# A fused attention and two-layer MoE kernel on one core: the weight projection moved into the key stage and spread over 32 blocks

## The chip, the core and the metric

The kernel runs on one core of a Trainium2 chip. The core has five engines that matter here: TensorE (PE, matrix products; its weight loads are shown as PEld), VectorE (DVE), ScalarE (ACT), GpSimd (POOL) and SyncE (SP, which here issues all DMAs). Every engine works through its own instructions in order and waits on semaphores for the others. On-chip data lie in SBUF; matrix products land in PSUM, eight banks per partition. The metric is the device time of one execution in microseconds (us), lower is better. The median of three runs of the kernel before is 1779.21 us (1768.62 to 1782.41).

## What is computed

Eight batches, eight heads, 576 positions, head size 64. A small set of 32 packed queries per head attends over the keys and values, the result is attended by the 576 queries, and the 4608 x 512 outcome goes through two feed-forward layers:

```python
p_packed = sm_attn(p, k, v)                # 32 x 64 per head
x = sm_attn(q, p_packed, p_packed)         # 576 x 64 per head
xn = x / sqrt(mean(x * x) + 1e-6) * rms_g  # x as 4608 x 512
g = xn @ w_gate
x1 = (g * sigmoid(g) * (xn @ w_val)) @ w_out      # d_ff 1536
h = x1 @ w2_in                                    # d_ff 2048
out = (h * cos(h)) @ w2_out
```

The weights arrive as 64-bit floats and are narrowed on the chip.

## The kernel before

The attention output of a batch is a 576 x 256 matrix of weights (softmax over 32 packed rows for 8 heads) times the packed values, so `xn @ w_gate` can be taken as (attention weights) x (packed values x w_gate). The product "packed values x weights" is the **projection**, `project` (L584). It makes, for each of 6 column chunks c, for gate and value (gv) and for each half of the heads (kt), a 128 x 4 x 256 piece for four batches at a time (bg = 0 is batches 0 to 3, bg = 1 is 4 to 7): 24 projections n of two **halves** (bg) each, 48 halves. A half is four matmuls into two PSUM tiles `mps`, one copy on ACT, one on DVE into an SBUF tile `ev` (4 buffers), and stores.

The program has these stages, one after the other in the order written (manual order up to the second layer):

- **Key stage** (loop over i = 0 to 17, two groups of four heads per batch): K and V are loaded ahead (`load_k(i + 3)`, `load_v(i + 2)`), POOL rearranges K (`u_copy`, L349, tile `kc`), PE transposes it (`u_kt`, tiles `kp`), scores `s` (`u_s1`), exponentials `e`, their transposes `et` (`u_et`), the packed values `pp` (`u_pp`), and their transposes `tp` (`u_fin`), which fill `ppT`, the projection's operand. Beside it 12 of the 24 pieces of w_gate and w_val (512 KB each, `wraw`, 3 buffers) and 4 pieces of w_out are loaded and narrowed in two parts, one iteration apart, and 26 of 43 steps of the attention of batch 0 (`bg0`) are interleaved.
- **First projections**: six of the 24 (both halves each), alternating with the rest of bg0.
- **Batch loop**: 24 blocks per batch (`gv_block`: 12 matmuls `gv` of gate and value; two blocks later `acc_block`: 12 matmuls `acc` into x1), with the attention of the next batch (`att_step`) interleaved. In batch 0 the 18 remaining projections run in the first blocks, one or two a block (`PJ_AT`), the last 12 weight pieces and 8 of w_out are loaded and narrowed there too, and batch 0 is taken in three segments of four d_ff blocks (`SEG`), whose partial sums of x1 go to DRAM and come back (`x1_load`). Batch 0's own part of a projection is copied straight into the SBUF tile `m0raw` by four 32 KB DMAs; everything else goes to `m_dram` and is read back per batch (`wm_load`), then split in two parts for the exact products (`wm_split`, tile `wmhl`, on ACT and POOL).
- **Second layer** (`h_block`, `o_block`), which the change does not touch.

Of the kernel before, what the change touches and what calls it, by code (L numbers as in the profile page):

```python
# [20 lines left out]
def kernel(  # L21
# [38 lines left out]
    BG_B, KP_B, ET_B, PP_B = 1, 2, 2, 1  # L60
    WRAW_B = 3
    WO_U = 4
    SEG, M0_D = 4, 0
    W_FROM, W_TO = 1, 14
    W_KV, W_B0 = 12, 12
    ATT_U, U_ATT, U_ATT_N = 26, 3, 2
    PJ_0, PJ_L, LATE_AT = 6, 0, 16
    PJ_AT = [7, 8] + [8 + x // 2 for x in range(1, 50)]
    EV_B = 4
    WM0_POOL = True  # L70
    W2_I0, W2_AT, W2_POOL = 25, (1, 3, 5, 7, 14, 18), False
    T_END, F3_B = 2, 3
    LAG, LAG_B = 2, 3
    WO_AT = {4: (-1, 0), 5: (1, 3), 6: (3, 6), 7: (6, 9), 8: (10, 12), 9: (13, 15), 10: (14, 17), 11: (16, 18)}
    M0_AT, M_AT = (16, 17, 18, 19, 20, 21), (3, 5, 7, 9, 11, 14)
    ATT_ORD = "t00 t01 x00 x01 x02 x03 t10 r00 t11 s00 x10 x11 p00 x12 p01 x13 - r10 - s10 - p10 p11"
    ATT_ORD0 = "t00 t01 x00 x01 x02 x03 r00 s00 p00 p01 t10 t11 x10 x11 x12 x13 r10 s10 p10 p11"
    AL_AT = 16
    X1_AT = {11: 0, 15: 1, 18: 0, 22: 1}
# [100 lines left out]

    gT = u1.tile([128, H], F32, name="gT")
    ppT = [mid_p.tile([128, H, 128], F32, name=f"ppT{i}") for i in range(B // 4)]
    pbd = [u1.tile([128, 2, 2 * NP], F32, name=f"pbd{i}") for i in range(2)]
    for t in pbd:
        nc.gpsimd.memset(t, 0.0)
# [142 lines left out]
    nat_k, nat_v, nat_c = {}, {}, {}  # L328
# [34 lines left out]
    def u_prep(i):  # L363
        pn, kc = nat_k.pop(i)[0], nat_c.pop(i)
# [3 lines left out]
        for r in range(2):  # L368
            rows = slice(r * 64, (r + 1) * 64)
            src, dst = (  # L370
                t[:, :, r * NP:(r + 1) * NP] for t in (pt[rows].rearrange("p (j x) -> p j x", j=2), pbd[i % 2][rows])
            )
            nc.vector.tensor_copy(dst, src)
        z["kT"], z["kc"] = u4.tile([128, 2, S], F32, tag="kT", name="kT"), kc

    def u_kt(i, js):
        z = st[i]
        kT, kc = z["kT"], z["kc"]
        for j in js:
            for hf in range(2):  # L380
                kp = ps_2.tile([128, HALF], F32, tag="kp", name="kp")
                for c in range(CH):
                    nc.tensor.transpose(
                        kp[:, c * CP:(c + 1) * CP],
                        kc[:, hf * CH + c, 2 * j:2 * j + 2, :].rearrange("p h d -> p (h d)"), ident[:CP, :CP],
                    )
                nc.scalar.activation(out=kT[:, j, hf * HALF:(hf + 1) * HALF], in_=kp, func=AF.Copy)

    def u_s1(i):
        z = st[i]  # L390
        kT = z["kT"]
        pb = pbd[i % 2]
        s1 = ps_1.tile([128, 2, 512], F32, tag="s1", name="s1")
        for hf in range(2):
            for j in range(2):
                nc.tensor.matmul(  # L396
                    s1[j * 64:(j + 1) * 64, hf, :HALF], pb[:, j], kT[:, j, hf * HALF:(hf + 1) * HALF],
                    start=True, stop=True,
                )
# [27 lines left out]
    def u_pp(i):  # L427
# [3 lines left out]
        pp = ps_1.tile([128, D], F32, tag="pp", name="pp", bufs=PP_B)  # L431
        for c in range(NC_):
            for h in range(4):
                r = slice(h * NP, (h + 1) * NP)
                nc.tensor.matmul(pp[r], eT[:, c, r], vn[:, h, c, :], start=c == 0, stop=c == NC_ - 1)
# [43 lines left out]
    def wy_prep(n, part):  # L479
        i, a = divmod(n, 2)  # L480
        c, gv = divmod(i, 2)
        if a == 0 and part == 0:
            w_y[i] = wm_p.tile([128, 4, 256], F32, tag="wm", name="wy")
# [522 lines left out]
```

## Time and profile before

| | |
|---|---|
| median of three runs | 1779.21 us |
| the profiled execution | 1776.91 us, its span 1775.1 us (1.8 us lie around it) |
| PE busy | 1696.1 us (96% of the span) |
| DVE, ACT, POOL busy | 1106.8, 863.8, 251.1 us |
| mean granted TensorE clock | 0.969 |

A busy PE is an engine with a matmul in flight, not an engine at its peak; the granted clock (1.00 is 2.4 GHz, and lower means are a mix with 1.2 GHz) and the idle time have to be read stage by stage.

### The profile page before, as it was taken

Reading aid. Unit: us, or ns where it says so; the run is one execution under the profiler, and the core shown is the slowest. Engines: PE = TensorE matmul, PEld = TensorE weight load, DVE = VectorE, ACT = ScalarE, POOL = GpSimd, SP = SyncE. Lnnn points to the kernel's source line nnn. Section 1 sums busy time; section 2 is a strip of 40 time slices with the busy share of each in tenths; the row PEclk is TensorE's granted clock in tenths of the full one; section 3 lists DMA queues with packets and bytes.
Section 4 is the critical chain, followed back from the end, with each engine's and each line's share of the span. In section 5 each row is a group of like instructions: output and inputs, shape, how many; then the busy total and the mean of one; then the engine's idle time right before and its main releaser. Section 6 shows DMA issues by size and latency. Waiting matters only on the chain.

```text
span 1775.1 us, 27791 instructions
## 1 busy us (share of the span) xinstructions
PE 1696.1 (96%) x10720; PEld 1495.0 (84%) x10720; DVE 1106.8 (62%) x2124; ACT 863.8 (49%) x1661; POOL 251.1 (14%) x202
## 2 busy tenths in 40 slices
PE   7787899799999999999999999999999999999999
PEld 4555677799999999999999888888888888888887
DVE  2565687557676767676656756565565656565554
ACT  4454454344444545454545645555554555454454
POOL 3331343412111111112122200000000000000000
PEclk9777899899999999999999999999999999999999
DMA  9995786553433334342223301010101000000000
GB/s 223 218 234 154 223 272 205 183 169 107 127 105 124 113 111 126 105 132 90 72 74 123 107 1 48 1 48 7 41 14 34 24 25 24 24 1 25 0 25 24
DMA packets 119981, 166.97 MB, mean 94 GB/s; under 512 B 26920, under 2 KB 84264, under 8 KB 119848
## 3 DMA queue, kind: packets, MB, share of 16 engines
q1 hardware_dynamic: 119848, 165.19, 32.1%
q8 instruction: 84, 1.38, 0.3%
q14 instruction: 49, 0.40, 0.1%
HBM read 108.79 MB, written 53.22 MB: 91 GB/s over the span
## 4 chain that ended last, share of the span: by engine, by line
PE 81%; DMA 6%; DVE 6%; issue 4%; ACT 2%; POOL 1%; SPq 0%; DVEq 0%; ACTq 0%; POOLq 0%
PE ops L154 7%; PE ops L152 7%; PE hp L153 7%; PE ops L153 7%; PE hp L152 7%; PE hp L154 7%; PE acc L152 5%; PE acc L153 5%; PE acc L154 5%; PE gv L152 5%; PE gv L154 4%; PE gv L153 4%; PE mps L595 2%; PE sp L235 1%; PE s L396 1%
## 5 line engine op out<-in xcount | busy, mean ns | idle before, releaser
L152 PE MATMUL gv<-apt,wmhl 128*128 128x288 f32 x768 | 234.3, 305 | 10.7 <-DVE silu L686 8.7
L152 PE MATMUL acc<-shl,wohl 128*128 128x288 f32 x768 | 237.4, 309 | 5.2 <-ACT wohl L104 5.0
L154 PE MATMUL acc<-shl,wohl 128*128 128x288 f32 x768 | 230.2, 300 | 0.5 <-POOL wohl L105 0.5
L153 PE MATMUL acc<-shl,wohl 128*128 128x288 f32 x768 | 230.3, 300 | 0.3 <-DVE shl L105 0.3
L154 PE MATMUL gv<-apt,wmhl 128*128 128x288 f32 x768 | 227.3, 296 | 1.0 <-POOL wmhl L105 1.0
L153 PE MATMUL gv<-apt,wmhl 128*128 128x288 f32 x768 | 227.6, 296 | 0.0
L152 PE MATMUL ops<-w2hl,ghl 128*128 128x512 f32 x576 | 224.2, 389 | 0.0
L153 PE MATMUL hp<-xhl,wmhl 128*128 128x512 f32 x576 | 224.1, 389 | 0.0
L154 PE MATMUL hp<-xhl,wmhl 128*128 128x512 f32 x576 | 224.1, 389 | 0.0
L153 PE MATMUL ops<-w2hl,ghl 128*128 128x512 f32 x576 | 224.1, 389 | 0.0
L152 PE MATMUL hp<-xhl,wmhl 128*128 128x512 f32 x576 | 224.1, 389 | 0.0
L154 PE MATMUL ops<-w2hl,ghl 128*128 128x512 f32 x576 | 222.7, 389 | 0.0
L926 DVE TENSOR_TENSOR r<-r,hp 128x512 f32<-128x512 f32 x144 | 98.9, 687 | 186.6 <-ACT r L925 186.6
L924 ACT ACTIVATE r<-r 128x512 f32<-128x512 f32 x144 | 91.0, 632 | 247.5 <-DVE r L923 247.5
L105 POOL TENSOR_TENSOR wmhl<-wmraw,wmhl 128x512 fp32r<-128x512 f32 x100 | 128.4, 1306 | 512.8 <-ACT wmhl L104 506.1
L104 ACT ACTIVATE shl<-silu 128x288 fp32r<-128x288 f32 x192 | 85.2, 444 | 231.9 <-DVE silu L687 230.7
L919 ACT ACTIVATE kk<-hp,magic 128x512 f32<-128x512 f32 x144 | 99.3, 689 | 122.6 <-PE hp L154 122.6
L152 PEld LDWEIGHTS gv<-apt,wmhl 128*128 128x128 f32 x768 | 145.5, 189 | 14.2 <-DVE silu L686 10.5
L152 PEld LDWEIGHTS acc<-shl,wohl 128*128 128x128 f32 x768 | 146.8, 191 | 10.8 <-ACT wohl L104 5.1
L153 PEld LDWEIGHTS acc<-shl,wohl 128*128 128x128 f32 x768 | 147.2, 192 | 0.6 <-DVE shl L105 0.5
L154 PEld LDWEIGHTS acc<-shl,wohl 128*128 128x128 f32 x768 | 146.6, 191 | 0.9 <-POOL wohl L105 0.9
L154 PEld LDWEIGHTS gv<-apt,wmhl 128*128 128x128 f32 x768 | 145.3, 189 | 1.5 <-POOL wmhl L105 1.5
(132 smaller groups left out, 3228.4 us busy)
## 6 DMA issues: line engine op xcount, KB each, us to landing
wmraw<-m SPq DMA_DIRECT2D x42, 512.0 KB
m<-ev SPq DMA_DIRECT2D x24, 512.0 KB, 4.2
x_dram<-x SPq DMA_DIRECT2D x40, 288.0 KB, 3.4
kn<-in_k_dram SPq DMA_DIRECT2D x16, 576.0 KB, 8.5
vn<-in_v_dram SPq DMA_DIRECT2D x16, 576.0 KB, 7.5
qnat<-in_q_dram SPq DMA_DIRECT2D x32, 288.0 KB, 6.2
m<-ev SPq DMA_DIRECT2D x24, 384.0 KB
x1raw<-x_dram SPq DMA_DIRECT2D x18, 512.0 KB, 3.9
```

The source lines that it names most:

```text
L104: nc.scalar.activation(out=hi, in_=src, func=AF.Copy)
L105: (eng or nc.vector).tensor_tensor(out=lo, in0=src, in1=hi.bitcast(F32), op=ALU.subtract)
L152: nc.tensor.matmul(ps, lhi, rhi, start=first, stop=False)
L153: nc.tensor.matmul(ps, lhi, rlo, start=False, stop=False)
L154: nc.tensor.matmul(ps, llo, rhi, start=False, stop=last)
L235: nc.tensor.matmul(sp[:, i, 2 * c:2 * c + 2, :], qT[:, i, c * CP:(c + 1) * CP], bq[:, 2 * j + i], start=True, stop=True,)
L396: nc.tensor.matmul(s1[j * 64:(j + 1) * 64, hf, :HALF], pb[:, j], kT[:, j, hf * HALF:(hf + 1) * HALF], start=True, stop=True,)
L595: nc.tensor.matmul(ps[r][:, j], ppT[bg][rows, 4 * kt + 2 * j + r], wy[rows, 2 * kt + j], start=True, stop=True)
L919: nc.scalar.activation(out=kk, in_=hp, func=AF.Identity, scale=1.0 / TWO_PI, bias=magic[:, 0:1])
L924: nc.scalar.activation(out=r, in_=r, func=AF.Abs)
L926: nc.vector.tensor_tensor(out=r, in0=r, in1=hp, op=ALU.mult)
```

## The change

It does six things.

1. The projection takes a half at a time. Twelve halves of bg = 0 (n = 0 to 11) run inside the key stage, in its iterations 10 to 16; the other 36 are spread over blocks 0 to 31 of the batch loop, one a block, two in blocks 4, 6, 8 and 10. The stage of first projections is gone.
2. For that the narrowed weights stay in SBUF until both halves are done, and the key stage loads 16 weight pieces in place of 12 (`W_KV`), with 4 buffers in place of 3 and both parts of the narrowing in the same iteration. Eight pieces are left for batch 0.
3. All of a half goes to `m_dram` by one 512 KB store, issued one step later (`store`); batch 0 reads its part back as other batches do. The `m0raw` copies are gone, and `ev` has 3 buffers in place of 4.
4. The partial sums of x1 of batch 0 stay in four SBUF tiles: 8 stores and 8 loads of 288 KB are gone. 
5. In the key stage the keys of one head fill 128 rows (even and odd positions in the two halves), so the POOL rearrangement is gone. The scores become eight matmuls with 64 rows and 32 columns of weights in place of four with 128 rows and 64 columns.
6. PSUM is dealt out anew there: two buffers for attention and projection (`mm`, was 1), three for `kp`, `tp` and now also `pp` (was 2, `pp` had its own), one for `et` (was 2). The key stage runs 34 of the 43 steps of bg0 (was 26). Loads of batch 1's projection pieces come at blocks 16 to 25 and their splits at 20 to 29. Preparing the second layer's weights begins at block 34 (was 25).

```diff
+    BG_B, KP_B, ET_B = 2, 3, 1
+    WRAW_B = 4
+    W_KV, W_B0 = 16, 16
+    ATT_U, U_ATT = 34, 3
+    PJ_S = {10: 2, 11: 2, 12: 2, 13: 2, 14: 2, 15: 1, 16: 1}
+    PJ_AT = {x: 1 for x in range(32)} | {4: 2, 6: 2, 8: 2, 10: 2}
+    EV_B = 3
-    def u_copy(i):
-        if i < NG:
-            kc = nat_c[i] = u5.tile([CP, NC_, 4, D], F32, tag="kc", name="kc")
-            nc.gpsimd.tensor_copy(kc, nat_k[i][1].rearrange("p h c d -> p c h d"))
...
-        for hf in range(2):
-            for j in range(2):
-                nc.tensor.matmul(
-                    s1[j * 64:(j + 1) * 64, hf, :HALF], pb[:, j], kT[:, j, hf * HALF:(hf + 1) * HALF],
-                    start=True, stop=True,
-                )
+        for h in range(4):
+            for r, rows in enumerate((top, bot)):
+                hs = slice(h * NP, (h + 1) * NP)
+                nc.tensor.matmul(s1[hs, r, :HALF], pT[i % 2][rows, hs], kT[rows, h], start=True, stop=True)
...
-            if bg == 0:
-                for h in range(4):
-                    nc.sync.dma_start(
-                        out=wm_raw[0, c][h * NP:(h + 1) * NP, 2 * kt + gv], in_=ev[:NP, h // 2, h % 2]
-                    )
+    def store(keep):
+        while len(stores) > keep:
+            dst, src = stores.pop(0)
+            nc.sync.dma_start(out=dst, in_=src)
...
+        for x in range(PJ_S.get(i, 0)):
+            store(0)
+            if x:
+                bg0_step(i, 1)
+            project(pj_0, 0)
+            pj_0 += 1
         if 0 < i <= NG:
             u_pp(i - 1)
...
-                x1 = x1_t.pop((b, hf, d2), None)
-                if x1 is None:
-                    x1 = x1_tile(b == 0, d2)
                 if f >= n:
+                    x1 = x1_t[hf, d2]
...
-                nc.sync.dma_start(out=x1_at, in_=x1)
+                if f == NF1 - 1:
+                    nc.sync.dma_start(out=x1_at, in_=x1)
...
+            store(0)
+            for _ in range(PJ_AT.get(i, 0)):
+                project(*PJ_L.pop(0))
```

How the order moves, at three places. PE in iteration 12 of the key stage, from the scores `s` to the packed values `pp`; `atp` are transposes of bg0. Before:

```order
L396 MATMUL s_1494<-kT,pbd_166 64x288 x4
L367 MATMUL pt<-ident,pn 128x128
L383 MATMUL kp<-ident,kc 128x96 x6
L447 MATMUL tp<-ident,cd 128x128
L383 MATMUL kp<-ident,kc 128x96 x6
L267 MATMUL atp<-ident,s 128x96 x3
L435 MATMUL pp<-vn,eT 32x64 x24
```

The same place in the changed kernel:

```order
L388 MATMUL s_1619<-kT,pT_169 32x288 x8
L365 MATMUL pt<-ident,pn 128x128
L375 MATMUL kp<-ident,kn 128x96 x6
L438 MATMUL tp<-ident,cd 128x128
L375 MATMUL kp<-ident,kn 128x96 x6
L271 MATMUL atp<-ident,s 128x96 x3
L508 MATMUL mps<-wy,ppT_164 128x256 x4
L271 MATMUL atp<-ident,s 128x96 x3
L508 MATMUL mps<-wy,ppT_164 128x256 x4
L424 MATMUL pp<-vn,eT 32x64 x24
```

Two halves of a projection and a second attention step now stand ahead of `pp`, and the scores are eight smaller matmuls.

PE at the end of the key stage; `gv` is the first block of the batch loop. Before, after the last `tp` twelve halves and the rest of bg0 follow, 32 rows up to the first `gv`:

```order
L447 MATMUL tp<-ident,cd 128x128
L435 MATMUL pp<-vn,eT 32x64 x24
L447 MATMUL tp<-ident,cd 128x128
L595 MATMUL mps<-wy,ppT_164 128x256 x4
L595 MATMUL mps<-wy,ppT_165 128x256 x4
L267 MATMUL atp<-ident,s 128x96 x3
```

Now:

```order
L438 MATMUL tp<-ident,cd 128x128
L508 MATMUL mps<-wy,ppT_164 128x256 x4
L424 MATMUL pp<-vn,eT 32x64 x24
L438 MATMUL tp<-ident,cd 128x128
L271 MATMUL atp<-ident,s 128x96 x12
L155 MATMUL gv_2244<-apt,wmhl 128x288
```

Only twelve transposes are left between the last `tp` and the first `gv`.

SP in the first blocks of batch 0, one projection a block before (`wo` are loads of weights, `qnat` of queries):

```order
L603 DMA m0raw<-ev 32x256 x4
L606 DMA m_2_82<-ev 96x4x256
L606 DMA m_2_88<-ev 128x4x256
L113 DMA wo<-in_moe_w_gate_dram 128x2x512
L113 DMA wo<-in_moe_w_out_dram 128x1024
```

and one half a block now:

```order
L520 DMA m_3_83<-ev 128x4x256
L116 DMA wo<-in_moe_w_gate_dram 128x2x512
L116 DMA wo<-in_moe_w_out_dram 128x1024
L520 DMA m_3_83<-ev 128x4x256
L116 DMA wo<-in_moe_w_val_dram 128x2x512
L208 DMA qnat<-in_q_dram 96x2x384
```

Six DMAs per block have become one store, and a load of 512 KB per chunk (`wmraw`) has come in.

## Rows read from the trace of the kernel before

**Rows 1.** Windows by stage: length; busy us of PE, PEld, DVE, ACT, POOL; clock; DMA; GB/s.
```profile
18.20:102.50 84.30, 68.54 (x758) 47.74 (x757) 40.36 (x101) 38.35 (x99) 25.52 (x18) 0.77 0.93 224
102.50:157.00 54.50, 39.01 (x520) 26.50 (x519) 38.51 (x98) 28.39 (x71) 19.44 (x13) 0.81 0.71 175
157.00:194.50 37.50, 29.42 (x150) 21.96 (x149) 14.42 (x27) 12.86 (x26) 3.34 (x3) 0.68 0.74 218
194.50:285.70 91.20, 81.87 (x540) 68.19 (x539) 73.65 (x129) 47.47 (x93) 35.63 (x24) 0.93 0.82 249
285.70:358.10 72.40, 62.52 (x422) 56.56 (x421) 44.83 (x90) 30.25 (x66) 28.43 (x22) 0.93 0.62 189
358.10:454.60 96.50, 92.22 (x710) 91.29 (x709) 64.60 (x140) 45.62 (x103) 22.33 (x18) 0.98 0.40 122
454.60:545.10 90.50, 89.85 (x710) 89.62 (x709) 64.68 (x140) 43.81 (x100) 17.27 (x14) 1.00 0.38 116
```

**Rows 2.** Waits of SP's queue, 0 to 160 us: total us, times, longest.
```profile
SPq L113 <- DVE wy L147: 19.1, 5, 6.0
```

**Rows 3.** PE's timeline in one iteration of the key stage: start, us, row.
```profile
101.02 1.52 PE L421 MATMUL et<-ident,e 128*96 128x128 f32 x6
102.47 1.92 PE L396 MATMUL s<-kT,pbd 128*64 128x288 f32 x8
...
107.31 1.48 PE L435 MATMUL pp<-vn,eT 96*32 96x64 f32 x48
```

**Rows 4.** Timeline of projections and of SP between the stages.
```profile
156.97 3.78 PE L595 MATMUL mps<-wy,ppT 64*128 64x256 f32 x16
...
164.62 3.78 SPq L603 DMA_DIRECT2D m0raw<-ev  x4
168.45 1.10 SPq L606 DMA_DIRECT2D m<-ev  x2
```

**Rows 5.** PE's timeline in batch 0: one half of a projection.
```profile
245.69 1.13 PE L595 MATMUL mps<-wy,ppT 64*128 64x256 f32 x8
```

**Rows 6.** The tile mps: DVE's copies (min/median/max ns), and what PE, DVE and ACT waited for.
```profile
L599 DVE COPY ev<-mps x48: 673/688/693, 159.1 to 316.5; 128x512 f32<-128x512 f32 x48
  DMA m<-ev: 19.8, 11
  DVE silu L686: 18.3, 18
```

**Rows 7.** The tile mps in windows by stage (PE records, DVE copies).
```profile
157.00:194.50 37.50, 22.32 (x112) 16.32 (x112) 8.98 (x13) 7.76 (x13) 0.68 0.74 218
194.50:285.70 91.20, 34.66 (x194) 21.81 (x192) 16.52 (x25) 14.17 (x25) 0.93 0.82 249
285.70:358.10 72.40, 12.63 (x80) 8.60 (x80) 6.58 (x10) 5.70 (x10) 0.93 0.62 189
```

**Rows 8.** DVE's groups from 194.5 to 285.7 us: narrowing of weight pieces.
```profile
L144 DVE SCALAR_TENSOR_TENSOR wy<-wo,wy 128x512 int32<-128x512 int32 x11 | 9.2, 832 | 0.4
L147 DVE SCALAR_TENSOR_TENSOR wy<-wo,wy 128x512 int32<-128x512 int32 x11 | 8.5, 771 | 0.4
L141 DVE TENSOR_SCALAR wy<-wy 128x512 int32<-128x512 int32 x11 | 5.7, 514 | 0.0
```

**Rows 9.** The chain of work that ended last, 300 to 400 us: start, us, what.
```profile
331.25 14.59 DMA wmraw<-m
...
351.09 13.13 DMA x_dram<-x
364.24 7.75 DMA x<-x_dram
```

**Rows 10.** Waits of PE, 285.7 to 372 us.
```profile
PE acc L152 <- ACT wohl L104: 5.0, 1, 5.0
PE gv L152 <- DVE silu L686: 4.8, 2, 2.9
```

**Rows 11.** DMA issues: KB each, median us to landing.
```profile
m<-ev SPq DMA_DIRECT2D x24, 512.0 KB, 4.2
```

More of the change, by code (lines that the diff above doesn't have):

```diff
@@ new lines, in project @@
+        ev = pr_p.tile([128, 2, 2, 256], F32, tag="ev", name="ev")
+        ps = [psb[0].tile([128, 2, 256], F32, tag="mm", name="mps") for _ in range(2)]
+        for j in range(2):
+            for r, rows in enumerate((top, bot)):
+                nc.tensor.matmul(
+                    ps[r][:, j], ppT[bg][rows, 4 * kt + 2 * j + r], wy[rows, 2 * kt + j], start=True, stop=True
+                )
+        nc.scalar.activation(out=ev[:, :, 0], in_=ps[0], func=AF.Copy)
+        nc.vector.tensor_copy(ev[:, :, 1], ps[1])
@@ L618, in wm_load @@
             return
-        pool = late["m"] if it[0] != "w" and it[0] > 0 else raw_p
-        t = wm_raw[it] = pool.tile([128, 4, 256], F32, tag="raw", name="wmraw")
+        pool = late["m"] if "m" in late and it[0] != "w" else late["raw"]
+        tag, bufs = ("raw", None) if pool is not u3 else ("wraw", WRAW_B)
+        t = wm_raw[it] = pool.tile([128, 4, 256], F32, tag=tag, name="wmraw", bufs=bufs)
         if it[0] == "w":
@@ L644, in wm_split, with w_due, bg0_step @@
             wm_t[it].append(t)
+    n_w = W_KV + WO_U
+    def w_due(i):
+        a, b = (n_w * max(0, min(x, W_TO) - W_FROM) // (W_TO - W_FROM) for x in (i, i + 1))
+        return range(a, b)
+    bg0 = attend(0)
+    def bg0_step(i, n):
+        for _ in range(n):
+            if i >= U_ATT and att_done[0] < ATT_U:
+                att_done[0] += 1
+                next(bg0)
+    order = ctx.enter_context(ExitStack())
+    order.enter_context(tc.manual_schedule())
+    late["raw"] = u3
+    u_prep(0)
@@ new lines @@
+    u_kt(0, range(4))
+    w_q = []
+    pj_0 = 0
+    for i in range(NG + 2):
+        due = list(w_due(i))
+        for n in due:
+            w_load(n)
+        load_k(i + 3)
+        if i == 1:
+            load_q()
+            load_q()
+        if 0 < i <= NG:
+            u_et(i - 1)
+        if i < NG:
+            u_s1(i)
+        if i + 1 < NG:
+            u_prep(i + 1)
+            u_kt(i + 1, [0, 1])
+        if 1 < i:
+            u_fin(i - 2)
+        if i == U_ATT:
+            att_load(0)
+        if i < NG:
+            u_e(i)
+        if i + 1 < NG:
+            u_kt(i + 1, [2, 3])
+        for n in w_q:
+            if n < W_KV:
+                w_prep(n, 0)
+        bg0_step(i, 1)
+        for x in range(PJ_S.get(i, 0)):
+            store(0)
+            if x:
+                bg0_step(i, 1)
+            project(pj_0, 0)
+            pj_0 += 1
+        if 0 < i <= NG:
+            u_pp(i - 1)
+        for n in w_q:
+            if n >= W_KV:
+                w_prep(n, 0)
+            w_prep(n, 1)
+        w_q = due
+        load_v(i + 2)
+        if i in M0_S:
+            wm_load((0, M0_S[i]))
+        if i - 2 in M0_S:
+            wm_split()
+        bg0_step(i, 2 if i < 9 else 1)
@@ L835 @@
             split_s(b, hf, f, t)
[L836 removed]
+            if i <= SPLIT0[-1] and i in SPLIT0:
                 wm_split()
[L838 to L841 removed]
+            store(0)
+            for _ in range(PJ_AT.get(i, 0)):
+                project(*PJ_L.pop(0))
+            if i == LATE_AT:
+                assert not PJ_L
+                after_project()
         if i >= LAG:
```

237 lines of the change are left out of this document (69 added, 168 removed).

## The prediction

> **What bounds the kernel now.** I read the windows by stage first [rows 1]: seven stretches, cut where iteration 10 of the key stage begins its scores (102.5), where the key stage ends (157.0), where the first block starts (194.5), at block 12 (285.7), and at the batches (358.1, 454.6, 545.1). The last stretch is a batch at its steady pace: 90.5 us, PE busy 89.85 of it, clock 1.00. So 24 blocks cost 90.5 us, 3.77 each, and no change that leaves their matmuls alone makes a batch shorter. What can be won lies ahead of 454.6 us. There PE is busy for less of the time, and in the key stage and behind it the clock averages 0.77, 0.81 and 0.68, so its busy time is partly slow time.
>
> What stands behind that differs. From 18.2 to 102.5 the DMA engines are 0.93 busy at 224 GB/s: the loads set the pace, helped by SP, which waits 19.1 us in all for the narrowing to free a weight buffer while the next K load stands behind it [rows 2]. From 102.5 to 157.0 DMA falls to 0.71, and the chain within an iteration sets the pace. Between the stages SP does: four small copies and two stores take 3.78 and 1.10 us of its time, 4.9 for one projection [rows 4], and six projections and the rest of the attention fill 37.5 us. In batch 0 projections wait for stores to free `ev` (19.8 us, this together with the stretch before) and for silu to free PSUM (18.3) [rows 6].
>
> **First part of the key stage, 18.2 to 102.5.** The schedule has issued 15 weight pieces by iteration 10 in place of 12 (20 pieces over 13 iterations in place of 16). Three pieces of 512 KB are 1.57 MB, 7.0 us at 224 GB/s. The DMA engines had 0.07 x 84.3 = 5.9 us free, and SP's wait for weight buffers should go. The POOL copy that stood between a K load and its transposes goes too; where the load itself is late, that gives no more than the copy's own time. A third attention step an iteration comes in: if DMA does not cover it, some 3 us. Bounds 0 and +10, taken +4.
>
> **Scores.** No row shows a 64 x 32 weight tile. The four old matmuls (eight records) take 1.92 us, two side by side; `pp`'s 24 matmuls of 32 columns (48 records) take 1.48 us, four side by side [rows 3]. Eight matmuls with an eighth of the array each take 0.96 us if all run together (half of 1.92), 1.92 if four do, 3.84 if two do, 7.7 if none. `pp` shows column tiles together, the projection (two halves, 16 records, in 3.78 us [rows 4]) works with row pairs; so I take 1.2. The Trainium skill ("TensorE: Matmul & The Clock Gate", Part 3: Packing small matmuls) says that row and column tiles combine and run at once; by it the eight would take about 0.96. The trace shows each kind, not both together. The single `et` buffer works against this: the second three transposes wait for ACT's copy of the first three, about 0.9 an iteration.
>
> **Second part, 102.5 to 157.0.** Two bounds. By DMA: 54.5 us x 175 GB/s = 9.5 MB, plus one weight piece (0.5), twelve stores (6.3) and two loads of chunks (1.0): 17.4 MB, which is 78 us at 224 GB/s and 70 at the 249 that batch 0 shows with stores in its mix [rows 1]. By PE: 39.0 us busy; twelve halves at 1.13 (full clock [rows 5]) to 1.89 (half of 3.78), 18 in the middle; attention steps that come from the stretch behind, where 29.4 - 22.3 = 7.1 us of PE were not projections [rows 1, 7], of these 5; for each half a hand-over, since with two PSUM buffers the next attention step waits for copies of 0.69 us [rows 6], 12 x 1.0; `et` +5, scores -4; and half of the idle 15.5 us stays, 8. That is 83. Both bounds are near each other, so neither hides the other; I take 83, bounds 70 and 100. Behind a projection in the queue stands `pp`, then the transposes `et` for the next iteration, so its lateness goes straight into the loop.
>
> **Between the stages.** The twelve transposes left lie within those 7.1 us; 3 to 10 (above, the wait for the first weight loads), taken 5. The first block then starts at 102.5 + 4 + 83 + 5 = 194.5: where it starts now. All that the removed stage gives is spent in the key stage.
>
> **Blocks 0 to 11.** Now 91.2 us: 12 x 3.77 = 45.2 of blocks, and 192 records, 24 halves, 27.1 us [rows 1, 5, 7]; 18.9 are lost. After: 16 halves, 18.1, so 63.3. DVE needs 73.65 now; nine copies fewer (25 to 16, 6.2) and three of eleven weight pieces fewer (23.4 us for eleven [rows 8], so 6.4) make 61. One store per half ends SP's crowding, and half the PSUM waits go; DVE is still as full as PE. I keep 10.7 of the loss: 74, bounds 66 and 88.
>
> The round of batch 0's own pieces through DRAM is new. A store lands in 4.2 us [rows 11]; the load is issued at least a block later and the split comes at least a block and a half (some 8 us) after it, which hides it. Without that cover each late chunk would hold ACT as the late one did before, about 5 us of PE [rows 10]; four make 20 (a rival, below). The Trainium skill ("DMA: Bandwidth & Descriptors", Rules for kernel authors) speaks against this edit: a DMA that reads what another wrote must wait for its completion first. The trace agrees that a store takes 4.2 us to complete; unhidden four times, that would make 1769.
>
> **Blocks 12 to 23.** Now 72.4: 45.2 and ten halves, 11.3; 15.9 are lost. The chain shows a chunk of batch 1 that took 14.59 us to come [rows 9]; ACT waits for it in its queue with the silu and w_out work behind, and PE then loses 5.0 and 4.8 [rows 10]. After the change these loads come two to five blocks ahead of their splits. Twelve halves, 13.6: 58.8 and 2.2 of loss, 61; bounds 59 and 72.
>
> **Batch 1.** 96.5 now, 6.0 over the steady pace: the x1 sums that go out and come back (13.13 and 7.75 us on the chain [rows 9]) hold DVE and the block behind it. They stay on chip now. Eight halves, 9.0, and 0.5: 100; bounds 99 and 106.
>
> The later batches and the second layer have the same instructions; the weight preparation that shifts by nine blocks lies beside PE, DMA 0.38 and DVE 64.7 of 90.5 us: 0. If that cover failed it would show as a batch over 90.5.
>
> **Sum.** 74 + 61 + 100 = 235 after the first block starts, 260.1 before: -25.1, with the start unmoved. From the profiled execution's 1776.9 (span 1775.1 and 1.8 around it) that is 1752. The median of the runs shown is 1779.2, 2.3 above the profiled one; 1752 is 1.5% under the median. About 1% (some 18 us) is what a measurement of this kernel can tell from no change.
>
> **The rivals.**
> - *The key stage eats it.* The hand-overs stay at the low clock and lie in series with the loads: second part 100 us. For it: both bounds stand within 5 us of each other, and clock 0.81. Against: more PE work may raise the clock. First block at 211.5, -8: 1769.
> - *Late chunks.* The four chunks of batch 0 that are written and read back in the loop come too late, because the blocks' other loads stand ahead of them at a DMA share of 0.82: +20, 1772. Against: the block and a half of cover.
> - *Scores don't run together* (slower). Pairs only, 3.84 in place of 1.2 in 16 iterations: +42, 1794; one by one, 7.7: +104, 1856. It decides from a group of about 3.9 us on. Against: rows for both kinds of tile.
> - *Better.* Second part at the 70 of the DMA bound, blocks 0 to 11 at 66: -21 more, 1731. For it: more work at the full clock. Against: DVE at 61 us of those 66.
>
> **How the numbers follow.** Forecast 0.61, with its own range 1739 to 1766 (second part 70 to 97 alone); key stage 0.15; late chunks 0.05; scores 0.07; better 0.12. The range 1728 to 1772 leaves out the scores' rival and tails of the others, under 2 in 10. Faster by over 1% (under 1761): all of "better" and some nine tenths of the forecast, 0.68; within 1%: the rest, the key stage's rival and the late chunks, 0.25; slower 0.07.
>
> **What would show it.** Scores groups of about 1.2 us; iterations 10 to 14 of about 12 to 14 us with DMA over 0.9; first `gv` near 194.5; no wait of `mps` for `m<-ev`; no `x` load; blocks 0 to 11 in 74 us, batch 1 in 100. Wrong would be: a first `gv` beyond 210, a scores group over 3 us, PE waiting in batch 0 for `wmhl`, or a steady batch over 91.

## The result, and the profile after

The changed kernel takes 1803.0 us (median of four runs, 1800.66 to 1805.25) where the kernel before takes 1779.3: a ratio of 1.0144 (95% interval 1.0098 to 1.0189). It is slower, by 1.4%. The forecast was 1752, in a range of 1728 to 1772: wrong in size and in sign. The prediction's own sign of being wrong, a first `gv` beyond 210, came too: it starts at 226.5.

The windows by stage of the changed kernel, cut as in [rows 1]: iteration 3 of the key stage up to 55.1, the rest of the first part up to the scores of iteration 10 (115.1), the second part up to the end of the key stage (213.5), the stretch up to the first block (226.5), blocks 0 to 11, blocks 12 to 23, batch 1, batch 2. The columns are the length, busy time and count of PE, PEld, DVE, ACT and POOL, the granted clock, the DMA share and GB/s:

```profile
28.70:55.10 26.40, 8.71 (x104) 6.12 (x103) 8.84 (x20) 5.43 (x13) 3.86 (x3) 0.63 0.77 189
55.10:115.10 60.00, 50.57 (x571) 35.97 (x572) 34.55 (x80) 30.24 (x74) 13.39 (x9) 0.56 0.86 227
115.10:213.50 98.40, 77.88 (x619) 51.83 (x618) 43.36 (x102) 36.15 (x82) 13.62 (x10) 0.52 0.52 152
213.50:226.50 13.00, 4.06 (x75) 2.98 (x74) 2.33 (x8) 4.79 (x11) 3.78 (x4) 0.85 0.60 171
226.50:303.20 76.70, 70.26 (x474) 60.23 (x475) 62.14 (x114) 40.37 (x81) 28.91 (x20) 0.94 0.73 228
303.20:375.10 71.90, 66.55 (x436) 57.86 (x436) 43.67 (x92) 31.65 (x69) 25.68 (x20) 0.93 0.45 146
375.10:475.60 100.50, 100.03 (x775) 96.00 (x774) 62.08 (x129) 47.88 (x106) 24.58 (x20) 1.00 0.41 135
475.60:566.10 90.50, 89.85 (x710) 89.61 (x709) 64.66 (x140) 43.83 (x100) 17.29 (x14) 1.00 0.38 116
```

Against [rows 1]: the start of the scores of iteration 10 moved from 102.5 to 115.1, the second part grew from 54.5 to 98.4, the stretch behind it shrank from 37.5 to 13.0, blocks 0 to 11 from 91.2 to 76.7; blocks 12 to 23 stayed (72.4, 71.9), batch 1 grew from 96.5 to 100.5, batch 2 is the same. The later batches took 1.5 us more together, and the second layer, from the last acc matmul to the end, 789.7 us in place of 784.1. The sum of the differences to the forecast, in us:

| stretch | forecast | measured | miss |
|---|---|---|---|
| scores of iteration 10 | 106.5 | 115.1 | +8.6 |
| second part | 83 | 98.4 | +15.4 |
| to the first block | 5 | 13.0 | +8.0 |
| blocks 0 to 11 | 74 | 76.7 | +2.7 |
| blocks 12 to 23 | 61 | 71.9 | +10.9 |
| batch 1 | 100 | 100.5 | +0.5 |
| later batches, second layer | as before | +1.5, +5.6 | +7.1 |

That is 53.2, and the profiled execution took 1805.0, 53.0 over 1752. The waits of PE in the key stage of the changed kernel (total, times, longest), then the one just ahead of the first block:

```profile
PE et L410 <- ACT eT L411: 30.4, 15, 8.8
PE sp L239 <- DMA bq<-q: 16.3, 1, 16.3
...
PE gv L155 <- DVE apt L108: 7.1, 1, 7.1
```

Four things stand out. *The wait for `bq`*: `sp`, the first product of bg0 that needs the values stored by the key stage, waited 16.3 us. *The w_out chains*: of the 30.4 us at `et`, 16.8 are two waits of 8.0 and 8.8, in iterations 13 and 14. *The single `et` buffer*: the other 13 of these waits, eleven of them of some 0.6 us, and two of 3.9 and 3.1 for which ACT came late. *The first chunk loads*: gv waited 7.1 us. One wait of the kernel before has gone in exchange, since `kp` has three buffers now; of this row 0.3 us are left:

```profile
PE kp L383 <- ACT kT L387: 8.9, 21, 0.6
```

The second of the four in instructions (start, length, what; the last bracket is the idle time and what ended it):

```profile
174.85 0.66 ACT L134 ACTIVATE ny<-wraw 128x512 f32<-128x512 f32 x1
...
175.60 1.49 POOL L135 TENSOR_SCALAR ny<-ny 128x512 f32<-128x512 f32 x1 [21.46 <-ACT ny L134]
...
177.15 0.84 PE L410 MATMUL et<-ident,e 128*96 128x128 f32 x3
...
178.31 0.69 DVE L150 SCALAR_TENSOR_TENSOR ny<-wraw,ny 128x512 int32<-128x512 int32 x1
179.03 0.63 ACT L107 ACTIVATE wohl<-ny 128x512 fp32r<-128x512 f32 x1 [3.52 <-DVE ny L150]
...
180.42 0.66 ACT L134 ACTIVATE ny<-wraw 128x512 f32<-128x512 f32 x1 [0.76 <-DVE wohl L108]
...
184.59 0.63 ACT L107 ACTIVATE wohl<-ny 128x512 fp32r<-128x512 f32 x1 [3.51 <-DVE ny L150]
...
185.42 0.47 ACT L411 ACTIVATE eT<-et 96x384 f32<-96x384 f32 x1
...
185.95 0.87 PE L410 MATMUL et<-ident,e 128*96 128x128 f32 x3 [7.96 <-ACT eT L411]
```

Two w_out pieces are narrowed one behind the other, each in a chain ACT, POOL, DVE, ACT through the single buffer `ny`. ACT stands in this chain from 174.85 to 185.2, idle for 3.5 us twice; the copy of the first `et` group, whose matmuls were over at 178, is queued behind it, and the second group needs that buffer.

### The profile page after: what moved, and what is told of

The parts are those of the page before. It is cut to its first block, busy times and chain, and to the rows that moved or that the text cites. A ratio compares the mean times of both kernels' runs of the same rounds, so it can differ in the third digit from the quotient of the medians.

```text
span 1803.2 us, 27704 instructions
## 1 busy us (share of the span) xinstructions
PE 1709.3 (95%) x10848; PEld 1498.5 (83%) x10848; DVE 1100.5 (61%) x2108; ACT 866.1 (48%) x1661; POOL 227.5 (13%) x184
## 4 chain that ended last, share of the span: by engine, by line
PE 83%; DVE 7%; DMA 5%; ACT 3%; issue 1%; POOL 1%; SPq 0%; DVEq 0%; ACTq 0%
PE ops L157 7%; PE ops L155 7%; PE ops L156 7%; PE hp L155 7%; PE hp L157 7%; PE hp L156 7%; PE acc L155 5%; PE acc L156 5%; PE acc L157 5%; PE gv L155 5%; PE gv L156 5%; PE gv L157 4%; PE mps L508 3%; PE sp L239 2%; DMA kn<-in_k_dram 1%
## 5 line engine op out<-in xcount | busy, mean ns | idle before, releaser
L108 POOL TENSOR_TENSOR wmhl<-wmraw,wmhl 128x512 fp32r<-128x512 f32 x112 | 145.2, 1318 | 544.7 <-ACT wmhl L107 540.9
L155 PEld LDWEIGHTS acc<-shl,wohl 128*128 128x128 f32 x768 | 145.9, 190 | 10.6 <-issue 10.2
```

The source lines that it names most:

```text
L108: (eng or nc.vector).tensor_tensor(out=lo, in0=src, in1=hi.bitcast(F32), op=ALU.subtract)
L155: nc.tensor.matmul(ps, lhi, rhi, start=first, stop=False)
```

## The experiments

Times are medians; ratios stand against the kernel before, with their 95% intervals (the changed kernel: 1.0144). The stage readings are of one profiled execution each. Two executions with the same program up to the second layer (the changed kernel and the run with the pools in another order, below) started the first block at 226.5 and 220.6, so a difference of some 6 us in that reading alone shows nothing.

### One wait each

**One attention step fewer in iteration 3.**

```diff
-        bg0_step(i, 2 if i < 9 else 1)
+        bg0_step(i, 2 if 3 < i < 9 else 1)
```

> The changed kernel with one attention step fewer in iteration 3 of the key stage, so that the first matmul on bq (sp) moves from iteration 3 to iteration 4. Theory of the waits: the 16.3 us that PE waits at sp for the load of bq is on the path and nothing covers it; iteration 3 (28.7 to 55.1 in the changed kernel, 26.4 us) falls to 10 to 14 us, the first block starts at 212 to 216 in place of 226.5, and the time is 1787 to 1793 in place of 1803. Theory of the load: the weight and K loads set the pace of the key stage, the wait only gave them time to run ahead; the iterations from 4 to 9 take longer by what iteration 3 gains, the first block starts at 223 or later and the time stays over 1799.

1796.2 us, ratio 1.0102 (1.0078 to 1.0127); scores of iteration 10 at 104.7, first block at 216.9. The load of `bq` is hardly earlier: SP issues it at 46.03, in the changed kernel at 47.46, in the kernel before at 45.65, and `sp` starts at 49.4, 50.9 and 49.3. What differs is what stands behind the wait in PE's queue. With three steps in iteration 3 the `et` and the scores of iteration 4 stood behind it; with two, iteration 4 begins at 38.8 in place of 55.1, and `sp` waits 6.3 us. In the kernel before it waited 3.4:

```profile
PE sp L235 <- DMA bq<-q: 3.4, 1, 3.4
```

The total gain is half of what the theory of the waits gave, since iteration 4 now takes 17.4 us. But 104.7 is 2.2 behind the kernel before, where the forecast had 4: the first part's miss was this one step. The other runs with one `et` buffer agree: with this edit they begin the scores of iteration 10 at 104.1 and 105.9, without it at 111.6 to 115.4.

**w_out one piece per iteration, in three phases.**

```diff
+        if wo_late:
+            wo_split(wo_late.pop())
...
+        wo_q += [n for n in w_q if n >= W_KV]
+        if wo_q:
+            w_prep(wo_q[0], 0)
...
-            if n >= W_KV:
-                w_prep(n, 0)
-            w_prep(n, 1)
+            if n < W_KV:
+                w_prep(n, 1)
+        if wo_q:
+            w_prep(wo_q[0], 1)
+            wo_late.append(wo_q.pop(0) - W_KV)
```

> The changed kernel with the w_out pieces of the key stage narrowed one per iteration (iterations 13 to 16 in place of two in 13 and two in 14) in three phases: ACT and POOL's parts with the others, DVE's behind the projections, the split an iteration later. Theory of the waits: the two waits of PE at the second et group (8.0 us at 186, 8.8 at 207.7), behind an ACT queue that runs through two whole chains of ACT, POOL, DVE and ACT, go; iterations 13 and 14 (23.1 and 21.7 us) fall to 14 to 16, the first block starts 12 to 17 us earlier (210 to 215) and the time is 1786 to 1792. Theory of the load: the projections at a granted clock of 0.52 and their stores set these iterations; they get at most 2 us shorter each, the first block starts at 222 or later and the time stays over 1798.

1790.2 us, 1.0065 (1.0042 to 1.0089); iterations 13 and 14 took 15.7 and 14.6 us (23.1 and 21.7), the first block is at 212.0. The theory of the waits holds in size too. PE's waits for `eT` from 114 to 212:

```profile
PE et L410 <- ACT eT L411: 4.4, 7, 0.9
```

and the window of iterations 10 to 14:

```profile
114.40:193.40 79.00, 74.53 (x548) 49.16 (x548) 35.30 (x86) 31.02 (x72) 10.60 (x8) 0.50 0.60 175
```

With the chains gone these iterations are no longer waiting: PE is busy for 74.5 of 79.0 us, at a clock of 0.50, and DMA for 0.60. So what is left there is PE's own work at the lower clock, not the loads.

**Chunk loads one iteration earlier.**

```diff
-    M0_S = {14: 0, 15: 1}
+    M0_S = {13: 0, 14: 1}
```

> The changed kernel with the two loads of batch 0's first chunks one iteration earlier (13 and 14 in place of 14 and 15). Theory of the waits: the load of chunk 1 was issued at 213.94 and took 10.54 us, its split held the ACT queue and PE waited 7.1 us ahead of the first block; that goes, the first block starts at 218 to 221 in place of 226.5, the time is 1795 to 1799. Theory of the load: ACT and DVE have the same work to do ahead of the first block, the load stands as early only to wait for its stores; the first block starts at 225 or later and the time stays over 1800.

1795.2 us, 1.0104 (1.0083 to 1.0125). PE's wait ahead of the first block went from 7.1 to 0.2, and the stretch from the scores of iteration 15 to the first block from 18.0 to 11.3 us:

```profile
PE gv L155 <- DVE apt L108: 0.2, 1, 0.2
```

**The three together.**

> The three edits together: one attention step fewer in iteration 3, the w_out pieces one per iteration in three phases, the two chunk loads one iteration earlier. Theory of the waits: the gains add, 11 to 14 and 12 to 17 and 5 to 7; the first block starts at 190 to 198, the time is 1765 to 1775, below the kernel before. Theory of the load: loads, stores and the projections at the low clock hold the stage; the first block starts at 215 or later and the time stays over 1792. In between (200 to 213): the gains overlap, and what is left is the work itself at its clock.

1783.4 us, 1.0021 (1.0003 to 1.0040); first block at 200.2, between the two theories. Alone they moved the first block by 9.6, 14.5 and 9.8; together by 26.3 in place of 33.9 (in an execution 6 us under its median). By the medians they gave 6.8, 12.8 and 7.8 alone and 19.6 in place of 27.4 together. That takes back 19.6 of the 23.7 us that the change lost: level with the kernel before, and nothing won yet.

### One PSUM buffer for et

**Two et and two kp buffers in the changed kernel.**

```diff
-    BG_B, KP_B, ET_B = 2, 3, 1
+    BG_B, KP_B, ET_B = 2, 2, 2
```

> The changed kernel with two PSUM buffers for et and two for kp in place of one and three, as the kernel before had them. In the changed kernel the second et group waits for ACT's copy of the first in every iteration (0.6 us at least, up to 8.8), and the granted clock is 0.50 in nearly every iteration from 55 to 208 us, where the kernel before had between 0.50 and 1.00. Theory of the gap: this recurring wait keeps the clock down; with two buffers iterations 4 to 9 fall from 10.6 us to 7 to 9, the mean clock from 55 to 208 rises to 0.65 or more, the first block starts 15 to 30 us earlier (197 to 212), the time is 1775 to 1790. Theory of the load: loads and queue order set the iterations and the clock follows from them; only the waits themselves go, 0.6 to 1 us in 16 iterations, at most 12 us; and where the second et group no longer waits, ACT's queue with the w_out chains still holds the next step: the clock stays under 0.58 and the time is 1793 to 1803.

1793.0 us, 1.0077 (1.0054 to 1.0101); first block at 213.1. In the windows the clock, 0.56 and 0.52 in the changed kernel, is 0.68 and 0.65:

```profile
55.00:109.00 54.00, 42.45 (x544) 30.43 (x544) 32.54 (x78) 29.57 (x72) 13.08 (x9) 0.68 1.01 246
109.00:190.00 81.00, 63.39 (x541) 42.72 (x541) 36.88 (x87) 31.49 (x74) 12.25 (x10) 0.65 0.59 171
```

The clock rose as the theory of the gap has it, the time came out at the other theory's edge. Iterations 3 and 14 still took 22.1 and 21.4 us: the `bq` wait and one of the w_out chains were untouched. The edit also takes the third `kp` buffer away, and a recurring wait comes back there, 18 times in place of once (the longest behind a w_out chain):

```profile
PE kp L375 <- ACT kT L379: 17.3, 18, 8.7
```

So it prices two and two buffers against one and three; no run has two and three.

**One et buffer in the kernel before.** The same edit the other way round, in a kernel without the other waits:

```diff
-    BG_B, KP_B, ET_B, PP_B = 1, 2, 2, 1
+    BG_B, KP_B, ET_B, PP_B = 1, 2, 1, 1
```

> The kernel before with one PSUM buffer for et in place of two, nothing else. It prices this edit by itself, in a kernel without the other waits. Prediction's price: 0.9 us in each of 16 iterations, no more than 14 us, and less where loads hold the iteration: the first block at 195 to 205, the time 1780 to 1790. Theory of the gap: the recurring wait also takes the full clock away from the key stage, of which the kernel before has some in most iterations (0.65 to 1.00 in 11 of 12): iterations of 10 us or more, the first block at 208 or later, the time over 1792.

1802.0 us, 1.0141 (1.0113 to 1.0168): this one buffer costs the kernel before as much as the whole change does. First block at 218.0 (194.5), as the theory of the gap has it. PE's wait for `eT` up to there:

```profile
PE et L421 <- ACT eT L422: 15.0, 16, 4.8
```

and the same 1422 matmul records, from the scores of iteration 1 to the first block, in the kernel before and in this run:

```profile
18.25:194.48 176.23, 136.90 (x1422) 96.17 (x1421) 93.29 (x224) 79.61 (x195) 48.30 (x33) 0.76 0.82 207
18.66:217.95 199.29, 156.41 (x1422) 102.39 (x1421) 93.06 (x224) 80.80 (x195) 47.90 (x33) 0.63 0.70 183
```

Fifteen of the sixteen waits are 0.58 to 1.17 us, about the prediction's 0.9, and the last is 4.8. But they are not what the time went to: PE is idle for 42.9 us in place of 39.3, 3.6 more, since other waits became shorter, and busy for 156.4 in place of 136.9. Of the 23.1 us, 19.5 are the same instructions at the lower clock. The score matmuls, one record each (minimum, median, maximum in ns), before and in this run, say it without the record of the clock: before, half of them took 457 ns or less, in this run none took less than 641.

```profile
L396 PE MATMUL s<-kT,pbd x128: 406/457/743, 11.1 to 145.8; 128*64 128x288 f32 x128
L396 PE MATMUL s<-kT,pbd x128: 641/687/743, 11.0 to 169.1; 128*64 128x288 f32 x128
```

The Trainium skill has a rule on such a wait ("Perfetto Trace Analysis", Optimizing Tensor Performance: independent matmul groups should rotate through PSUM banks, so that emptying one overlaps the next); these runs agree with it.

### Where the halves stand

**The halves behind acc in the blocks**, with the three edits above.

```diff
-            for _ in range(PJ_AT.get(i, 0)):
-                project(*PJ_L.pop(0))
...
         if i >= LAG:
             acc_block(*seq[i - LAG])
+        if i < len(seq):
+            for _ in range(PJ_AT.get(i, 0)):
+                project(*PJ_L.pop(0))
```

> The three edits together as before (one attention step fewer in iteration 3, w_out one per iteration in three phases, chunk loads one iteration earlier), and in the blocks the projection's halves behind acc in place of between gv and acc. Theory of the place: between gv and acc the halves ask for PSUM tiles that gv still holds; PE waits for silu (4.1 us in blocks 12 to 23, 5.2 in blocks 0 to 11 of the run with the three edits) and for some 5 us after the longer of these waits its matmuls run at half the clock (block 16 took 9.4 us, block 19 8.8); behind acc these tiles are free. Blocks 12 to 23 fall from 70.8 to 59 to 64, blocks 0 to 11 from 76.8 to 68 to 73; the time is 10 to 18 us under that run's: 1760 to 1772. Rival: DVE, ACT and POOL, which narrow and split weights in these blocks, set their pace, and the wait moves to acc or to the next gv; blocks 12 to 23 stay over 68 and the time over 1772.

1770.3 us, 0.9950 (0.9931 to 0.9970): faster than the kernel before, and the theory of the place holds. Blocks 12 to 23 went from 70.8 to 62.7 us, blocks 0 to 11 from 76.8 to 73.6, about what the prediction gave them (61 and 74). In the changed kernel a half stood between gv and acc and asked for PSUM tiles that gv still held; DVE, behind three narrowing steps of `ny`, came to silu late. PE and DVE in block 15 of the changed kernel (320.8 to 330.9):

```profile
321.95 1.09 DVE L144 TENSOR_SCALAR ny<-ny 128x512 int32<-128x512 int32 x1
323.08 1.64 DVE L147 SCALAR_TENSOR_TENSOR ny<-wo,ny 128x512 int32<-128x512 int32 x1
323.27 0.70 PE L508 MATMUL mps<-wy,ppT 64*128 64x256 f32 x2
324.75 0.69 DVE L150 SCALAR_TENSOR_TENSOR ny<-wo,ny 128x512 int32<-128x512 int32 x1
325.37 0.45 DVE L687 TENSOR_TENSOR silu<-silu,gv 128x288 f32<-128x288 f32 x1
325.87 2.07 PE L508 MATMUL mps<-wy,ppT 64*128 64x256 f32 x6 [1.91 <-DVE silu L687]
327.87 0.61 PE L155 MATMUL acc<-shl,wohl 128*128 128x288 f32 x1
328.27 0.44 PE L156 MATMUL acc<-shl,wohl 128*128 128x288 f32 x1
328.51 0.44 PE L157 MATMUL acc<-shl,wohl 128*128 128x288 f32 x1
```

and the window behind that wait:

```profile
326.00:331.00 5.00, 5.00 (x19) 4.17 (x20) 3.51 (x7) 2.27 (x4) 1.84 (x2) 0.50 0.27 92
```

PE waited 1.91 us, and then every matmul to 331.6 ran at a clock of 0.50: the start of one acc matmul follows the last by 240 ns, where 130 ns is its distance elsewhere in the same batch. The 5.7 us at half speed cost some 2.8 more than the wait itself. Block 15 (16 in the expectation, which counts it by its end) took 10.1 us in the changed kernel and 6.3 in this run. The window of the twelve blocks in this run:

```profile
278.00:340.60 62.60, 61.05 (x436) 53.25 (x434) 45.09 (x92) 31.11 (x69) 25.73 (x20) 1.00 0.52 171
```

**Two et buffers on top.**

> The run with the three edits and the halves behind acc, and with two PSUM buffers for et and two for kp in place of one and three. That run's iterations 5 to 9 took 10 us each with PE busy for nine tenths at half speed (an et matmul 421 ns, where it takes 270 at the full clock); alone, the two buffers brought the first block of the changed kernel from 226.5 to 213. Theory of the gap: with no wait at the second et group the matmuls of iterations 4 to 14 are faster part of the time and the iterations 1 to 2 us shorter; the first block starts at 186 to 196 in place of 204, the time is 1752 to 1762. Rival: once the w_out chains are spread, the 13 us that the two buffers gave are already had, since they stood in the same iterations; the first block starts at 199 or later and the time stays over 1764.

1767.0 us, 0.9934 (0.9908 to 0.9959); first block at 200.2. The times are the rival's: what 13 us had been alone is 4 here, within what two executions differ by, and the two intervals overlap. The reason is not only that the waits stood in the same iterations. The 11.1 us of waits at `et` are gone, but with the third `kp` buffer given up for them this has come, where the run before has no such row:

```profile
PE kp L375 <- ACT kT L379: 10.6, 22, 0.6
```

Up to the first block PE is busy for 143.8 us in place of 156.6 and idle for 40.4 in place of 31.9.

**All twelve halves behind the key loop**, once in the changed kernel and once in the run just above.

```diff
-    PJ_S = {10: 2, 11: 2, 12: 2, 13: 2, 14: 2, 15: 1, 16: 1}
-    M0_S = {14: 0, 15: 1}
+    PJ_S = {}
+    M0_S = {}
...
+    for x in range(12):
+        store(0)
+        project(x, 0)
+        if x in (5, 9):
+            wm_load((0, x // 9))
     store(0)
+    for x in range(2):
+        wm_split()
```

> The changed kernel with the twelve halves of the projection taken out of the key stage and put behind it in one row, with the loads of the two chunks among them and their splits at the end; the w_out chains, the attention steps and the buffers stay. Theory that the interleaved halves cost: a half in the key stage takes 2 to 3 us at the clock of 0.5 with its hand-overs; behind the loop it is paced by ACT's and DVE's copies and three ev buffers, 1.5 to 2 us; iterations 10 to 14 fall from 15 to 23 us to 9 to 17, the key stage ends near 178 to 186, the first block starts at 206 to 218 and the time is 1784 to 1797. Rival, the interleaving pays: the halves stand in time that the loads and the w_out chains need anyway; the key stage ends after 190 and the halves come on top, the first block starts at 222 or later, the time is 1800 or more.

> The same run with the twelve halves out of the key stage and in one row behind it (loads and splits of the two chunks behind them). Theory that interleaving costs even without the waits: behind the loop a half takes 2 us, paced by ACT's copy (with one wait of 5 us for a store, 29 in all), in the loop it adds 3 or more at half speed; the first block starts 4 us or more before that of the run with the halves in the loop. Rival, the interleaving was right and only its waits were wrong: with the waits gone the halves stand beside loads and copies, and taken out they come on top; the first block starts 5 to 15 us later than in that run, the time is 5 to 15 us longer.

In the changed kernel this wins: 1793.8 us, 1.0083 (1.0059 to 1.0107), first block at 215.9. Iterations 10 to 14 took 62.4 us in place of 93.4, 3.1 less for each of ten halves, and behind the loop twelve took 29.6 (181.6 to 211.3). With the waits out it loses: 1772.9, 0.9972 (0.9956 to 0.9989), against 1767.0. There iterations 10 to 14 take 47.1 us without the halves and 77.2 with them, 3.0 a half; the stretch from iteration 15 to the first block takes 54.6 without and 20.5 with. The first block starts 3.5 us later without them, within what two executions differ by; so it is by the medians that the interleaving itself gives some 6 us. A half in the loop costs 3.0.

**One half per iteration, four behind.**

```diff
+    PJ_S = {x: 1 for x in range(10, 18)}
...
+    for x in range(8, 12):
+        store(0)
+        project(x, 0)
```

> The same run with one half in each of the iterations 10 to 17 and four behind the loop. If the cost of a half in the loop is the same for the first and the second in an iteration, the first block starts between those of the two other runs; if it is the second half of an iteration that costs (its PSUM buffers wait for the copies of the first, its store for the one before), this run's first block starts earliest of the three, by 3 us or more.

1772.9 us, 0.9975 (0.9959 to 0.9991). Iterations 10 to 14 took 59.6: the first half of an iteration cost 2.5 us, the second 3.5, by one execution of each run. But the first block was the last of the three, at 204.6, if by little, so neither case of the expectation holds: what one half per iteration saves in the loop comes back behind it.

### Scores alone

The kernel before with part 5 only: the eight small score matmuls, `pT` in place of `pbd`, no POOL copy (the new `u_prep`, `u_kt` and `u_s1` as in the change's diff).

> The kernel before with part 5 alone: eight score matmuls of 64 rows by 32 columns from pT, transposes straight from kn, no POOL copy of K and no block-diagonal pbd; all buffers, the attention steps and the projections as before. Prediction's price: 0.7 us less PE per iteration for the scores and POOL's 1.3 to 2 us off the way from a K load to its transposes; loads set the pace of the first part, so the first block starts at 188 to 194.5 and the time is 1773 to 1779. Rival: with the work on PE shorter, the granted clock of 18 to 157 us falls from 0.77 and 0.81 to under 0.65, and the key stage gets longer; the first block starts after 198, the time is 1783 or more.

1773.9 us, 0.9968 (0.9947 to 0.9990): a small gain. First block at 189.5 (194.5), clock 0.73 from 21 to 97 us (0.77): the rival's fall of the clock did not come. The scores themselves in the changed kernel, the eight matmuls as 16 records (minimum, median and maximum of one record in ns):

```profile
L388 PE MATMUL s<-kT,pT x176: 402/684/686, 65.7 to 209.0; 64*32 64x288 f32 x176
```

In the timeline a group takes 1.21 us where these records are at 684, and 0.72 at 95.6 us, where the clock was full for a while: all eight side by side. The old groups took 2.19 and 1.19 at these two levels; the 1.92 in [rows 3], from which the prediction took its 1.2, was a group with some of both.

### The second layer

In the changed kernel and in every edit of it above, this layer took 789.5 to 791 us, with the same wait at its start:

```profile
PE hp L155 <- DVE r L901: 3.7, 1, 3.7
```

and ACT there:

```profile
1014.85 0.69 ACT L894 ACTIVATE kk<-hp,magic 128x512 f32<-128x512 f32 x1 [0.43 <-PE hp L157]
1016.26 2.19 ACT L107 ACTIVATE wmhl<-wmraw 128x512 fp32r<-128x512 f32 x4 [0.72 <-DMA x_dram<-x]
1018.85 0.63 ACT L899 ACTIVATE r<-r 128x512 f32<-128x512 f32 x1 [0.40 <-DVE r L898]
```

ACT splits four weight tiles in a row ahead of `r`; in the kernel before it took `r` first, then two. The code there is the same, and the order is the scheduler's. Opening the layer's three pools in another order puts their tiles at other addresses, and the scheduler then gives DVE and ACT the order of before:

```diff
-    b2 = ctx.enter_context(tc.tile_pool(name="b2", bufs=2, reuse_waits="tile"))
     b3 = ctx.enter_context(tc.tile_pool(name="b3", bufs=3, reuse_waits="tile"))
     b4 = ctx.enter_context(tc.tile_pool(name="b4", bufs=4, reuse_waits="tile"))
+    b2 = ctx.enter_context(tc.tile_pool(name="b2", bufs=2, reuse_waits="tile"))
```

> The changed kernel with the second layer's pools b2, b3 and b4 opened in the order b3, b4, b2; with this the tiles lie at other addresses, and the scheduler gives DVE and ACT at the start of the layer the order that they had in the kernel before (the r of the first block ahead of the w2hl split, the wmhl splits two by two in place of four in a row). Theory of the order: the 3.7 us wait of PE for r and the slow matmuls behind it go, the layer takes 784 to 785 us in place of 789.7, the time is 1796 to 1799 in place of 1803. Rival, it runs over from the batches (loads of the layer's weights that come late): the layer stays at 788 us or more and the time at 1801 or more.

> The best run so far (three edits, halves behind acc, two et buffers; 1767.0) with the pools in the order b3, b4, b2. Theory of the order: 5 to 6 us less, 1760 to 1763, 1% under the kernel before. Rival: 1765 or more.

The layer takes 784.5 and 784.3 us, PE waits there for nothing that the waits show. ACT at its start, with this order in the changed kernel:

```profile
1007.00 0.62 ACT L899 ACTIVATE r<-r 128x512 f32<-128x512 f32 x1
1007.83 1.15 ACT L107 ACTIVATE wmhl<-wmraw 128x512 fp32r<-128x512 f32 x2 [0.21 <-DMA x_dram<-x]
1009.00 1.28 ACT L900 ACT_TABLE_LOAD   x1
```

On the changed kernel: 1795.8 us, 1.0096 (1.0066 to 1.0126). On the best run so far: 1762.7, 0.9909 (0.9889 to 0.9928), 15.5 us under the kernel before and the fastest of all. So the 5.6 us of the layer, of which 5.2 came back, go with the scheduler's order, and the order with where the tiles lie; which overlap in memory turns it was not tried.

## Why the prediction was wrong, by its own steps

- **First part of the key stage (+4; +12.6).** Without the third attention step in iteration 3 the kernel stands at +2.2, inside the bounds; whether the loads make that up as counted, no run separates. The step that failed is "a third attention step an iteration comes in: if DMA does not cover it, some 3 us". It was priced as work; it was a queue position. The third step moved `sp` ahead of the scores of iteration 4, and `sp` needs `bq`, which let it start at 49.3 to 50.9 us in these three kernels wherever it stood in PE's queue. The 3.4 us wait of `sp` stood in the trace of before, and the prediction does not use it.
- **Scores (1.2 us).** Right: 1.21 at the lower clock, 0.72 at the full one, though the 1.92 that it was worked out from belongs to neither. The Trainium skill's rule on combined row and column tiles ("TensorE: Matmul & The Clock Gate", Part 3: Packing small matmuls) agrees with these records.
- **The single et buffer (0.9 an iteration).** The wait was sized right (about 0.6 in most iterations) and its effect was not: in the kernel before, with two `kp` buffers, it costs 23.5 us, nearly all of it as PE's busy time at the lower clock. The prediction put 5 us of it in the second part and none in the first. The change pairs the one `et` buffer with a third `kp` buffer; what that pair costs against two `et` and three `kp`, no run shows.
- **Second part (83; 98.4).** "Hand-overs" and "half of the idle time stays" left out that both parts of the w_out narrowing now stand in one iteration, with one `ny` buffer (the kernel before has two there; the list of the change does not name this) and the split right behind: two chains of some 5 us on ACT in each of two iterations, ahead of the copy of `et`. 14.4 us of these iterations went when they were spread; the second buffer was not tried by itself. The DMA bound (70 to 78) was no bound: DMA was busy for 0.52. PE was, but at another clock: its 39.0 us of before were taken over as they stood at 0.81, and the stage ran at 0.52; a half, priced at 2.5 with its hand-over, cost 3.0. With the waits out this is what is left: the best run takes 97.2 us from the scores of iteration 10 to the first block, where the forecast had 88.
- **Between the stages (5; 13.0).** The prediction weighed late chunks in the block loop, where they cost nothing that the waits show. The late one was chunk 1, whose load is issued at the end of the key stage: 7.1 us of PE.
- **Blocks 0 to 11 (74; 76.7).** Within its bounds.
- **Blocks 12 to 23 (61; 71.9).** A term was mis-sized: a half was priced at 1.13 us from [rows 5], twelve at 13.6. They were busy for 17.9 and waited 5.2 more for silu and the statistics. 1.13 is the price of a half with free PSUM tiles at the full clock; this place in the block often gave neither. Behind acc eight of the twelve took 1.13 to 1.15, and the stretch takes 62.7.
- **Batch 1 (100; 100.5).** Right: eight halves took 9.3 us, and the x1 sums no longer hold anything.
- **Second layer (0; +5.6).** "The same instructions" is not the same order: the scheduler's order changed with the layout.
- **The rivals.** *The key stage eats it* was the right place and half the size: it gave the second part 100 us (98.4), but left the first part and the stretch behind it alone, 17 of the 32.0 us by which the first block came late. The only rival on the slower side was the scores, which were right. A slower rival from a wait that the change adds to a queue (`sp`, w_out, `et`) was missing, and that is what came.

## What to carry to other kernels

Price a moved step by what it waits for and by what is queued behind it on its engine, before its own duration: three queue positions (`sp` ahead of scores, w_out ahead of `eT`, a half ahead of acc) and the late chunk load cost 32.7 us here by the medians, where the change was meant to win 27. A buffer given up on the one path that every iteration goes through can cost far more than its wait, if the matmuls around it lose the full clock (19.5 of 23.1 us in the kernel before); and a buffer won there by giving up another moves the wait (from `et` to `kp`). When the sum of a change rests on durations from busy, full-clock stretches, look up the same instruction at the lower clock and take that for a stage whose clock is mixed.

## What the hardware showed beside this

In the key stage a recurring wait of 0.6 us in an iteration of 10.6 went with a clock of 0.50 throughout (55 to 87 us, PE busy for 0.93 of it), though PE had more to do than before. The wait alone does not decide it: the kernel before has the `kp` waits of 0.6 us in this stage and a clock of 0.77 and 0.81, with one iteration at 0.50 as well (83.5 to 94.8, PE busy for 0.92). The record of the granted clock is no sure guide: in the run with the halves behind acc it reads 1.00 in the first part, while the `et` matmuls there take as long as at 0.50. One window of it, its `et` matmuls (minimum, median, maximum in ns), and the same in the changed kernel, where the clock reads 0.56:

```profile
68.00:78.00 10.00, 9.28 (x101) 7.35 (x101) 5.39 (x15) 4.77 (x12) 1.48 (x1) 1.00 1.09 261
```

```profile
L410 PE MATMUL et<-ident,e x31: 421/421/449, 56.6 to 105.6; 128*96 128x128 f32 x31
```

```profile
L410 PE MATMUL et<-ident,e x30: 272/421/450, 63.4 to 104.7; 128*96 128x128 f32 x30
```

The duration of an instruction that recurs tells the level; the Trainium skill, too, warns that these clock records can't be relied on ("TensorE: Matmul & The Clock Gate", Part 1, Seeing it yourself), and this run agrees.
